# Retention and Fourier mixing on one core: the hand-ordered first batch reworked

## The chip, the cores and the metric

The kernel runs on one core of a Trainium2 chip. The metric is the device time of one execution in microseconds (us). The kernel before takes 272.87 us (median of three runs, 272.81 to 275.85).

## What is computed

Four batches, eight heads, 768 positions, head width 64. A retention layer is followed by a Fourier mixing layer and an MLP. The reference, cut:

```python
for t in range(S):                       # retention, per head, gamma = 1 - 2**(-5-h)
    state = gamma * state + outer(k[:, :, t], v[:, :, t])
    y[:, :, t] = scale * q[:, :, t] @ state
x = y as (batch, 768, 512)
u = x + real(fft(fft(x, axis=1), axis=2))
un = (u - mean(u)) / sqrt(var(u) + 1e-6)
out = u + relu(un @ w_ch1) @ w_ch2       # 512 -> 2048 -> 512
```

## The kernel before

**Retention.** The 768 positions are six chunks of 128 (`NCH`). Heads go in pairs, in the order of `PAIR_ORDER`. For each pair the kernel transposes q and k on TensorE, multiplies them chunk by chunk (`wkA`), applies the decay mask (`atm`), builds the states between chunks (`wkK`, `s16`), adds both parts in PSUM (`wkY`) and writes x as f16. Head columns 0 to 255 go to one side of `xts`, 256 to 511 mirrored to the other, with edge columns of zeros.

**Fourier mixing.** The two transforms are done as real products with cosine and sine tables. `fold_s` adds and subtracts the two halves of the positions (`xab`); `fold_d` adds and subtracts the two sides (`eo`, index e for sum and difference, cb for a half of the columns); `s1_unit` is the first DFT step (six matmuls for each e and cb, then one copy to `g`, on ACT or VectorE); `g0_unit` computes one extra column that is added as a scalar per row; `gr_unit` makes the mirrored copy `g16r`; `s2_unit` is the second DFT step for a block of 128 rows (kb 0 to 5). It leaves the cosine part (psP) and the sine part (psQ) in one PSUM bank, copies psQ to `qn` on ACT, combines them on VectorE into `u` (two instructions, L708 and L710), and adds x in two halves (L714, L717). Blocks 3 to 5 use the mirrored `g`. `norm_unit` subtracts the mean. For blocks 0 to 2 of batch 0 the mean comes from a sum of x (`xmean_unit`) and g0 (`mean_unit`), so that the statistics can wait.

**MLP.** `unT_unit` transposes the block (TensorE for batches 0 and 1, a DMA transpose for 2 and 3), `h_unit` (L778) or, for the first three blocks of batch 0, `h0_unit` (L795) is the first product with its ReLU, `ch_unit` (L815) the second. The MLP of one batch (the list `majors`) is interleaved with the retention and DFT of the next.

**What sets the order.** `first_units` is a list written by hand for batch 0's retention, DFT and first normalised blocks. After each of its units `pin()` ties every new instruction to the last one of its engine, so every engine runs the list in this order. After that `emit` merges streams of units, each with a start and an end on an axis on which the MLP of batch b covers b to b + 1. The units before 0.05 are pinned on all engines, the later ones on Pool alone; on the other engines the framework's scheduler orders them. `late_consts` (the masks `maskp`, eight ACT copies) is emitted between the two.

**Around the change.** On Pool the start sets decay constants (`gk5`, L185 and L287), edge columns (L277, L278) and casts q, k and v of each pair (L328, L337, L340, L353). `csn_unit` (L244) copies a cosine table for g0. `parity_consts` is six small VectorE instructions. `filler(n)` (L115) issues n matmuls on zeros to keep TensorE active. `sc_unit` is the scan over chunks (L425), `ae_unit` the masks (L401), `x0_unit` the write of x (L469). `load_unit(1, i, after)` lets batch 1's loads wait for a weight load. PSUM has five banks for most tiles (`ps_g`), two for the retention output (`ps_y`) and one for fillers (`ps_w`) in the first part; then three banks take the place of the last two for `psh` and `psc` (`ps_pm`).

## Time and profile before

| | us or share |
|---|---|
| time, median | 272.87 |
| profiled span | 270.6 |
| first MLP matmul (L795) starts | 41.2 |
| TensorE busy | 90% |
| VectorE busy | 70% |
| ScalarE (ACT) busy | 42% |
| GpSimd (POOL) busy | 29% |
| filler matmuls L115 | 41, 13.6 us |
| last load of batch 0 issued, landed | 14.9, 22.2 |

A row of the page's groups gives line, engine and operation, written and read tiles with shapes and count, then busy time and mean ns of one, then the idle time of the engine just before and what ended it. A line of the timeline starts with its start and its length; a group that was merged has a count (x4). A line of the waits gives who waited for whom, then total us, times and the longest. PEld is TensorE's weight load, SPq the queue from which loads and stores are issued.

### The profile page before, as it was taken

Reading aid. Unit: us, or ns where it says so; the run is one execution under the profiler, and the core shown is the slowest. Engines: PE = TensorE matmul, PEld = TensorE weight load, DVE = VectorE, ACT = ScalarE, POOL = GpSimd, SP = SyncE. Lnnn points to the kernel's source line nnn. Section 1 sums busy time; section 2 is a strip of 40 time slices with the busy share of each in tenths; the row PEclk is TensorE's granted clock in tenths of the full one; section 3 lists DMA queues with packets and bytes.
Section 4 is the critical chain, followed back from the end, with each engine's and each line's share of the span. In section 5 each row is a group of like instructions: output and inputs, shape, how many; then the busy total and the mean of one; then the engine's idle time right before and its main releaser. Section 6 shows DMA issues by size and latency. Waiting matters only on the chain.

```text
span 270.6 us, 5220 instructions
## 1 busy us (share of the span) xinstructions
PE 244.0 (90%) x2009; PEld 147.3 (54%) x2009; DVE 188.7 (70%) x447; ACT 114.0 (42%) x232; POOL 78.7 (29%) x138
## 2 busy tenths in 40 slices
PE   7785775989999989999997899999999999999994
PEld 2364554875666544666554544665566446545541
DVE  8996848599988874699776672798787725623421
ACT  4885456375464542356224540451144413502300
POOL 8987125556000053454000390170002401200000
PEclk9998589999999999999999999999999999999999
DMA  8999997999989985979983044159110231112012
GB/s 183 264 244 146 202 203 149 253 218 249 185 203 203 190 134 146 235 145 220 212 193 79 1 87 128 39 108 146 39 41 0 51 107 39 38 42 78 0 41 78
DMA packets 97432, 35.99 MB, mean 133 GB/s; under 512 B 88192, under 2 KB 94336, under 8 KB 97408
## 3 DMA queue, kind: packets, MB, share of 16 engines
q1 hardware_dynamic: 93184, 31.47, 55.9%
q0 software_dynamic: 4224, 4.19, 9.8%
q8 instruction: 16, 0.26, 0.4%
q14 instruction: 8, 0.07, 0.1%
HBM read 27.26 MB, written 6.29 MB: 124 GB/s over the span
## 4 chain that ended last, share of the span: by engine, by line
PE 48%; DVE 30%; ACT 6%; DMA 6%; POOL 5%; issue 3%; SPq 0%; POOLq 0%; ACTq 0%; DVEq 0%
PE psc L815 22%; PE psh L778 14%; DMA qTz<-q16z 4%; DVE bst L734 4%; POOL u L717 3%; PE ps L645 3%; DVE atm L401 3%; DVE u L708 2%; ACT x L591 2%; DVE ht L784 2%; DVE u L710 2%; DVE eo L618 1%; DVE tmp L233 1%; DMA v<-in_v_dram 1%; PE psh L795 1%
## 5 line engine op out<-in xcount | busy, mean ns | idle before, releaser
L815 PE MATMUL psc<-w,ht 128*128 128x512 f16 x384 | 90.1, 379 | 0.0
L778 PE MATMUL psh<-unT,w 128*128 128x384 f16 x448 | 83.3, 326 | 2.4 <-DVE ht L784 1.4
L778 PEld LDWEIGHTS <-w 128*128 128x128 f16 x448 | 42.7, 98 | 27.9 <-issue 4.9
L815 PEld LDWEIGHTS <-ht 128*128 128x128 f16 x384 | 36.6, 98 | 36.6
L782 ACT ACTIVATE ht<-psh 128x384 f16<-128x384 f32 x56 | 27.3, 488 | 56.6 <-PE psh L778 56.6
L714 POOL TENSOR_TENSOR u<-u,x 128x256 f32<-128x256 f32 x18 | 11.4, 634 | 125.6 <-DVE u L708 123.3
L819 DVE SCALAR_TENSOR_TENSOR ob<-psc,stats,u 128x512 f32<-128x512 f32 x24 | 17.9, 745 | 30.5 <-PE psc L815 30.5
L784 DVE TENSOR_SCALAR ht<-psh 128x384 f16<-128x384 f32 x56 | 30.7, 548 | 11.3 <-PE psh L778 11.2
L532 DVE TENSOR_TENSOR atm<-wkA,maskp 128x512 f16<-128x512 f32 x36 | 24.0, 681 | 1.0 <-PE wkA L530 1.0
L736 ACT ACTIVATE un<-u,stats 128x512 f16<-128x512 f32 x21 | 15.2, 722 | 18.4 <-DVE stats L735 13.9
L591 ACT ACTIVATE x<-wkY,gexp 128x384 f16<-128x384 f32 x24 | 12.7, 581 | 20.4 <-PE wkY L583 20.4
L734 DVE BATCH_NORM_STATS2 bst<-u 128x6 f32<-128x512 f32 x21 | 14.5, 691 | 7.6 <-POOL u L717 7.6
L717 POOL TENSOR_TENSOR u<-u,x 128x256 f32<-128x256 f32 x21 | 13.6, 646 | 15.4 <-DVE u L714 10.6
L558 DVE SCALAR_TENSOR_TENSOR s<-s,gk,wkK 128x128 f16<-128x128 f16 x48 | 16.3, 339 | 1.0
L708 DVE SCALAR_TENSOR_TENSOR u<-pq,g,qn 128x257 f32<-128x257 f32 x24 | 11.5, 477 | 5.9 <-ACT qn L705 5.9
L313 POOL TENSOR_SCALAR kd<-k,gexp 128x384 f16<-128x384 f32 x24 | 13.8, 585 | 4.8 <-DMA k<-in_k_dram 4.8
L795 PE MATMUL psh<-unT,w 128*128 128x128 f16 x192 | 11.9, 219 | 3.7 <-DVE ht L802 3.4
L115 PE MATMUL wps<-ht 128*128 128x512 f16 x41 | 13.6, 448 | 1.4 <-POOL ht L156 1.4
L795 PEld LDWEIGHTS <-w 128*128 128x128 f16 x192 | 11.2, 98 | 4.3 <-issue 4.2
L530 PE MATMUL wkA<-qTz,kT 128*128 128x256 f16 x72 | 13.3, 273 | 0.2
L311 ACT CAST q16z<-q 128x384 f16<-128x384 f32 x16 | 7.7, 513 | 10.9 <-DMA qTz<-q16z 10.9
L710 DVE SCALAR_TENSOR_TENSOR u<-pq,g,qn 128x255 f32<-128x255 f32 x24 | 11.2, 468 | 0.0
(138 smaller groups left out, 325.4 us busy)
## 6 DMA issues: line engine op xcount, KB each, us to landing
q<-in_q_dram SPq DMA_DIRECT2D x16, 384.0 KB, 6.1
k<-in_k_dram SPq DMA_DIRECT2D x16, 384.0 KB, 5.1
v<-in_v_dram SPq DMA_DIRECT2D x16, 384.0 KB, 6.0
out_dram<-ob SPq DMA_DIRECT2D x24, 256.0 KB, 2.3
w<-in_moe_w_ch_dram POOLq DMA_DIRECT2D x8, 512.0 KB, 10.9
unT<-un SPq DMA_TRANSPOSE x12, 2.4
qTz<-q16z SPq DMA_TRANSPOSE x8, 4.8
kT<-kd SPq DMA_TRANSPOSE x8, 2.8
```

Of the source, the lines that this page charges most:

```text
L532: nc.vector.tensor_tensor(out=st["atm"][:, 2 * part:2 * part + 2], in0=wk, in1=maskp[:, PAIR_ORDER[i]].unsqueeze(1).to_broadcast([P, 2, 2, ...
L591: nc.scalar.activation(dst, yk[h2], AF.Copy, bias=0.0, scale=gq8[:, h:h + 1])
L708: nc.vector.scalar_tensor_tensor(out=u[:, kb, 0:257], in0=psP, scalar=g0, in1=qn, op0=ALU.add, op1=op_lo)
L710: nc.vector.scalar_tensor_tensor(out=u[:, kb, 257:512], in0=psP[:, 255:0:-1], scalar=g0, in1=qn[:, 255:0:-1], op0=ALU.add, op1=op_up)
L717: eng.tensor_tensor(out=u[:, kb, 256:512], in0=u[:, kb, 256:512], in1=x[:, kb, 1, 257:1:-1], op=ALU.add)
L734: nc.vector.bn_stats(bst, u[:, kb, :])
L778: nc.tensor.matmul(psh, w116[:, cb, fb * P:(fb + 1) * P], unT[:, cb, rt * 384:(rt + 1) * 384], start=(cb == 0), stop=(cb == 3))
L782: nc.scalar.activation(ht16[:, fb, :], psh, AF.Relu, bias=0.0, scale=-1.0)
L784: nc.vector.tensor_scalar(out=ht16[:, fb, :], in0=psh, scalar1=-1.0, scalar2=0.0, op0=ALU.mult, op1=ALU.max)
L795: nc.tensor.matmul(psh[:, f], w116[:, cb, fb * P:(fb + 1) * P], unT[:, cb, kb * P:(kb + 1) * P], start=(cb == 0), stop=(cb == 3))
L815: nc.tensor.matmul(psc, ht16[:, fb, rb3 * P:(rb3 + 1) * P], w216[:, fb, :], start=(fb == 0), stop=(fb == NFB - 1))
L819: nc.vector.scalar_tensor_tensor(out=ob, in0=psc, scalar=lb[b]["st"][:, rb, 3:4], in1=lb[b]["u"][:, rb, :], op0=ALU.mult, op1=ALU.add)
```

## The change

It reworks the hand-written first batch and moves a few things in the streams:

- [...]The memsets of the decay constants `gk5` on Pool become ACT copies from a small VectorE table `gkrow` (which also takes the place of `gk128`). The zeros of `qTz` move from Pool to VectorE and later. `csn_unit` goes to a later place, the edge columns of the second x tile to the end of the list.
- **Residual of the first blocks on TensorE.** For blocks 0 to 2 of batch 0, `px_unit` adds x in the PSUM of the second DFT step: four matmuls with half an identity (`hid`, `nhid`), since psP + psQ and psP - psQ give both sides. The edge columns of `qn` get half of x by a small ACT copy. The adds L714 and L717 are gone for these blocks. For blocks 3 to 5 of batch 0 the adds move from VectorE to Pool.
- **g0 chain split.** `g0_unit` is in three parts: its input copies, its matmuls, its last two VectorE instructions, each in its own place.
- **Order.** `fold_d` is split by e, pair 3's masks for head 0 come ahead of the scan, more fillers stand there, means are taken per block, two mirror copies come earlier, the copy of g for e = 1 is always on VectorE.
- **Streams.** Batch 1's loads wait for the seventh weight load, not the eighth. Batch 1's retention starts at 0.27 of batch 0's MLP, not at 0.12. In all batches the first step's second columns and the second step are placed later. Pool is pinned only before 1.0.

The core of the diff:

```diff
     def gk_unit(hp):
         def run():
-            for h2 in range(2):
-                nc.gpsimd.memset(gk5[D * h2:D * h2 + D, hp, :, 1:NCH - 1],
-                                 float(gam[2 * hp + h2] ** P))
+            nc.scalar.copy(gk5[:, hp], gkrow[:, hp].unsqueeze(1).to_broadcast([P, D, NCH - 1]))
...
     def qt_zeros():
         for j in range(2):
-            nc.gpsimd.memset(qts[j][0:D, 1], 0.0)
-            nc.gpsimd.memset(qts[j][D:P, 0], 0.0)
+            nc.vector.memset(qts[j][0:D, 1], 0.0)
+            nc.vector.memset(qts[j][D:P, 0], 0.0)
...
+    def px_unit(kb):
+        def run():
...
+            pq = lb[0]["pq", kb] = (ps_y if kb < 2 else ps_g).tile(
+                [P, DM], f32, tag="y" if kb < 2 else "g", name="pq0")
+            x = xts[0][:, kb]
+            for n, (dst, half, side, lo, hi) in enumerate((
+                    (pq[:, 0:257], hid, 0, 1, 258), (pq[:, 0:257], hid, 1, 1, 258),
+                    (pq[:, 257:512], hid, 0, 2, 257), (pq[:, 257:512], nhid, 1, 2, 257))):
+                nc.tensor.matmul(dst, half, x[:, side, lo:hi], start=(n == 0), stop=False,
+                                 skip_group_check=True)
...
+            if early:
+                nc.scalar.activation(
+                    qn[:, 0:257:256],
+                    xts[0][:, kb].rearrange("p s d -> p (s d)")[:, 1:XW + 258:XW + 256],
+                    AF.Copy, bias=0.0, scale=0.5)
             nc.scalar.copy(qn[:, 1:256], psQ)
...
-            eng = nc.vector if b == 0 else nc.gpsimd
-            eng.tensor_tensor(out=u[:, kb, 0:256], ...)
-            eng = nc.vector if (b == 0 and kb >= 3) else nc.gpsimd
-            eng.tensor_tensor(out=u[:, kb, 256:512], ...)
+            if early:
+                return
+            nc.gpsimd.tensor_tensor(out=u[:, kb, 0:256], ...)
+            nc.gpsimd.tensor_tensor(out=u[:, kb, 256:512], ...)
...
-        un += a(3) + [kv0_unit(3), sc_unit(3)] + e(3, *heads)
-        un += [yx_unit(3), filler(1), yi_unit(3, 0), x0_unit(3, 0), yi_unit(3, 1), x0_unit(3, 1),
-               t_act(4, 1), t_act(4, 2)]
-        un += [fold_s(0, 0, 130, 1, 2), fold_d(0, 0), g0_unit(0), s1_unit(0, 0, 0),
-               s1_unit(0, 1, 0), filler(2), xmean_unit(0)]
-        un += [fold_s(0, 130, 258, 1, 2), fold_d(0, 1), s1_unit(0, 0, 1), s1_unit(0, 1, 1),
-               filler(2), xmean_unit(1), xmean_unit(2), mean_unit]
-        un += [s2_unit(0, 0), s2_unit(0, 1), norm_unit(0, 0), filler(6), unT_unit(0, 0),
-               s2_unit(0, 2), norm_unit(0, 1), norm_unit(0, 2)]
-        un += [gr_unit(gi) for gi in range(4)] + [gk_late]
+        un += a(3) + e(3, (0, 0), (1, 0)) + [kv0_unit(3), filler(3), sc_unit(3),
+               t_act(4, 0), t_act(4, 1)]
+        un += e(3, (0, 1), (1, 1))
+        un += [yx_unit(3), yi_unit(3, 0), x0_unit(3, 0), filler(2), yi_unit(3, 1), x0_unit(3, 1),
+               g0_unit(0, (1,))]
+        un += [fold_s(0, 0, 130, 1, 2), fold_d(0, 0, (0,)), s1_unit(0, 0, 0), t_act(4, 2),
+               fold_s(0, 130, 258, 1, 2), fold_d(0, 0, (1,)), fold_d(0, 1, (0,)), px_unit(0),
+               xmean_unit(0), fold_d(0, 1, (1,)), s1_unit(0, 1, 0), s1_unit(0, 0, 1),
+               s1_unit(0, 1, 1), px_unit(1), filler(1), g0_unit(0, (2,)), mean_unit(0)]
+        un += [s2_unit(0, 0), s2_unit(0, 1), norm_unit(0, 0), gr_unit(0), gr_unit(1),
+               px_unit(2), filler(4), unT_unit(0, 0), xmean_unit(1), mean_unit(1),
+               norm_unit(0, 1), s2_unit(0, 2), xmean_unit(2), mean_unit(2), norm_unit(0, 2),
+               gr_unit(2), gr_unit(3), edge_zeros, x_edges(1)]
...
-            pin(None if e[0] < 0.05 else ["Pool", "GpSimd"])
+            if e[0] < 1.0:
+                pin(None if e[0] < 0.05 else ["Pool", "GpSimd"])
...
-                streams.append(([load_unit(1, i, 7) for i in range(4)], -0.1, 0.0))
-                streams.append(([qt_zeros], 0.02, 0.05))
+                streams.append(([load_unit(1, i, 6) for i in range(4)], -0.1, 0.0))
+                streams.append(([qt_zeros], 0.1, 0.15))
                 streams.append(([pad_unit], 0.9, 0.95))
-                ts = (0.12, 0.22, 0.24, 0.33, 0.42, 0.52, 0.59, 0.67)
+                ts = (0.27, 0.31, 0.34, 0.42, 0.51, 0.60, 0.67, 0.74)
...
-                ts = [0.04 + 0.58 * sum(n[:j]) / sum(n) for j in range(7)]
+                ts = [0.04 + 0.57 * sum(n[:j]) / sum(n) for j in range(7)]
...
-            streams.append((mix_units(b + 1, [0, 1, 2]), b + ts[-1], b + ts[-1] + 0.15))
+            streams.append(([s1_unit(b + 1, 0, 1), s1_unit(b + 1, 1, 1)], b + ts[-1] + 0.04,
+                            b + ts[-1] + 0.06))
+            streams.append((mix_units(b + 1, [0, 1, 2]), b + ts[-1] + 0.09, b + ts[-1] + 0.24))
```

## The prediction

> **What bounds the kernel now.** I read the page's busy shares and slices first, then TensorE's waits on both sides of 47 us, then the timeline of the stretches with the long waits. The page:
>
> ```profile
> PE 244.0 (90%) x2009; PEld 147.3 (54%) x2009; DVE 188.7 (70%) x447; ACT 114.0 (42%) x232; POOL 78.7 (29%) x138
> PE   7785775989999989999997899999999999999994
> PEclk9998589999999999999999999999999999999999
> ```
>
> A slice is 6.8 us. From the eighth on PE is at nine tenths or more nearly throughout; the first seven are looser, and only there does the granted clock fall. PE's waits before 47 us, then after 47 us:
>
> ```profile
> PE wkY L456 <- DVE s L425: 1.8, 2, 1.4
> PE pst L765 <- ACT un L730: 1.5, 1, 1.5
> PE ps L671 <- DVE xg L666: 1.5, 1, 1.5
> ```
>
> ```profile
> PE psh L795 <- DVE ht L802: 3.4, 1, 3.4
> PE pq L699 <- ACT g L650: 1.6, 1, 1.6
> PE pst L765 <- ACT un L736: 1.6, 3, 0.7
> ```
>
> So two regimes. Up to 47.8 us a dependency chain sets the time: loads, four head pairs, folds, DFT steps, first MLP matmul at 41.2. After it PE has work ahead; adding the idle of 5 us windows from 50 us on gives 8.0 us, of which only the waits above can be touched. The longest is in the timeline of 42 to 48 us:
>
> ```profile
> 42.56 3.73 DVE L658 COPY g16r<-g 128x384 f16<-128x384 f16 x4
> 43.08 0.73 POOL L207 MEMSET qTz<- 64x768 f16 x1
> ...
> 43.80 1.69 ACT L197 ACTIVATE maskp<-maskf 128x128 f32<-128x128 f32 x8
> ...
> 45.39 1.05 ACT L800 ACTIVATE ht<-psh 128x512 f16<-128x512 f32 x2
> ...
> 47.01 0.69 DVE L802 TENSOR_SCALAR ht<-psh 128x512 f16<-128x512 f32 x1
> 47.76 2.45 PE L795 MATMUL psh<-unT,w 128*128 128x128 f16 x41 [3.41 <-DVE ht L802]
> ```
>
> PE has filled three psh buffers and stands until VectorE, in its fixed order, is through four mirror copies and eight small memsets. The copies are slow:
>
> ```profile
> L654 DVE COPY g16r<-g x12: 247/261/264, 87.3 to 205.9; 128x384 f16<-128x384 f16 x12
> L658 DVE COPY g16r<-g x4: 867/869/1364, 42.6 to 45.4; 128x384 f16<-128x384 f16 x4
> ```
>
> The same copy takes 261 ns later, and 869 ns here, while Pool sets qTz.
>
> **What the Trainium skill says.** "SBUF — State Buffer", section "SBUF: two separate sides": VectorE in a two-port mode (or reading two SBUF tensors, against a Pool operation that reads) and Pool take one port pair as a lock for a whole instruction, the other blocks. The two rows agree: 261 against 869 ns. "TensorE: Matmul & The Clock Gate", Part 1: PE's clock halves after a window of about 3.4 us with too little activity, and comes back after a busy one. The trace agrees: the clock is 0.50 from 26 to 35 us after a thin stretch (PE busy 0.42, 0.30 and 0.76 in the windows at 22, 24 and 25 us), and six DFT matmuls take 1.07 to 1.18 us there against 0.67 at 138 us. How many fillers hold it, neither says.
>
> **The change part by part.**
>
> Start, 0 to 21 us. Off Pool go the gk memsets (0.76 + 1.53 + 1.48 us) and the csn copies; two ACT copies of 320 elements (about 0.45 us each, from 0.52 for 386) run before ACT's first trig input is there (5.14 now). The casts can then follow the loads (now kd of pair 0 waits for the gk memsets till 7.8, though k0 landed at 5.8), but loads set the last pair: k3 was issued at 14.35 and landed 6.8 us later, at 21.2; v3 at 22.2. DMA is busy at 1.0 or more throughout. Casting earlier brings pair 0 about 1.2 us and pair 1 about 1 us forward, and nothing of it survives at pair 3. The parity constants (2.2 us at 9.45) move ahead of pair 2's masks; VectorE has 2.1 us of idle before pair 3, which hides them. I cost this part at 0.
>
> Pair 3, 21 to 30 us. More fillers (ten for two between 22 and 29 us, 0.21 us each, in PE's idle time) push its kT by up to 0.4 us; head 0's two masks ahead of the scan let yi of head 0 go earlier. I put pair 3's last x at 29.9, as before (29.95). Gain 0.
>
> Folds and first DFT step, 30 to 36 us. Before, VectorE did fold 0.62, both differences 1.03, the g0 chain to 31.6, then fold 0.62 and 1.03, ending 33.2. Now one difference (0.52) comes ahead of the second fold, and the g0 copies are done long before: 29.95 + 0.62 + 3 x 0.52 = 32.1. So the last difference is 1.1 us earlier. PE's four groups of six cost 0.55 us each at full clock instead of 1.1. Four residual matmuls of 257 or 255 columns are added per block; PE streams 512 columns in 216 ns (48 in 10.36 us), so about 0.11 each, 0.45 a block, 1.3 in all, on a PE which waits for VectorE here. Last group 32.15 to 32.75, px(1) and a filler to 33.45 beside the copy of g (0.59), second step's matmuls done 34.0, against 36.8. **Gain 2.85 us if the clock holds; about 0 if it doesn't** (four groups at 1.1 and px at 0.9 a block end where they did). The nearest bounds on an unseen thing are these two. I take the first: the fillers between 22 and 29 us go from 0.4 to 2.1 us of PE work.
>
> Second step to first MLP matmul. Before: second-step matmuls end 36.8, first transpose 40.1, so 3.3 us. Gone are the VectorE add (0.41) and Pool's add with its handover (0.85); new is a two-element ACT copy per block (nearest rows 0.19 to 0.29; I take 0.2, behind PE's work). That leaves 2.4, and four fillers of 0.86 end ahead of it. Transposes at 36.4, first MLP matmul 37.5, against 41.2: 3.7 us by here.
>
> The stall at 44 us. Mirror copies 0 and 1 go earlier, 2 and 3 cost 0.26 each, the gk128 memsets (0.77) are gone, qTz memsets leave Pool for VectorE later (four of 0.22 to 0.43; the 192-word memset took 0.22). PE fills three buffers by 40.3. VectorE frees its one at about 42.0. The other two wait for ACT, which has un of block 1 (to 39.1), block 2's copies (39.7), the mean of block 2 (0.81), un (to 41.5), eight maskp copies (1.69, to 43.2) and then ht, to 43.8. So PE gets one group at 42.0 and stays busy from 43.9; before, the same group started at 47.76 and the one after it at 48.7. **Gain 4.8 us in all**: the stall does not go, ACT inherits 3.6 us of the gap; the gain is nearly all the 3.7 from above plus 1.1 here.
>
> Batch 0's later blocks: six adds of 0.41 to 0.66 leave VectorE for Pool at 0.64 each. Pool's order puts them ahead of batch 1's casts, whose loads now start when the seventh weight load has landed, about 42 instead of 44.8. Hidden while PE has MLP work. Batch 1's attention starts at 0.27 of the batch instead of 0.12 and ends at 0.74; VectorE, 89% busy from 50 to 95 us, takes its 26 us (per pair three mask products of 0.68, four state steps of 0.34, 0.28 and 0.96 of copies, 18.6 for four; some 7.5 of folds and g copies) in a narrower space. Slack: batch 1's last un was ready at 104, its first MLP matmul ran at 108.6. I cost it at 0, with 3 us as upper bound.
>
> Room between steps. Second columns' first step and the second step come 0.04 and 0.08 of a batch later. What it can recover is PE idle near these steps: 1.0 us at 95 to 105, 3.1 at 135 to 160, 0.9 at 200 to 215. The middle one:
>
> ```profile
> 147.75 0.51 ACT L311 CAST q16z<-q 128x384 f16<-128x384 f32 x1 [2.68 <-DMA qTz<-q16z]
> ...
> 148.95 0.59 ACT L650 CAST g<-ps 128x386 f16<-128x386 f32 x1
> ...
> 149.60 0.28 PE L699 MATMUL pq<-cd,g 128*128 128x257 f16 x1 [1.64 <-ACT g L650]
> ```
>
> The copy of g stands on ACT behind a cast that waits for a DMA transpose; spacing doesn't remove the cast. Of 5.0 us I take a quarter, 1.2; bounds 0 and 3.
>
> Sum: 4.8 + 1.2 = 6.0, so 272.9 - 6.0 = **266.9 us**.
>
> **Rivals.**
> Clock still drops: 2.85 us of the first part go, and half the room is gained: 272.9 - 2.0 - 0.6 = 270.3. For it: how much activity holds the clock is not shown. Against it: eight more fillers.
> VectorE or loads take it back in batch 1: loads start only 2.8 us earlier, so 4.8 falls to 2.8, and the compressed attention gives no room: 270.1. For it: VectorE's 89%. Against it: 4.6 us of slack at 104.
> Larger: all three DFT stalls go (3 of 5) and ACT's 3.6 us gap half closes because the order of maskp and ht differs: 272.9 - 4.8 - 3.0 - 1.6 = 263.5.
> Slower: Pool's order is no longer pinned from batch 1 on, so casts for the next batch may stand ahead of residual adds and wait for loads. One such wait is in the chain already (DMA of v, 3.79 us at 116.3, ahead of an add at 120.1). If it hit the two adds of three blocks, at two places in three batches, 6 x 3.8 = 23 less half hidden behind MLP work, less 4.8: 272.9 + 6.6 = 279.5. For it: ACT, not pinned, shows it at 147.75. Against it: the pinned order has the wait too, and PE lost only 0.2 us at 120.
>
> **How the numbers follow.** Forecast 0.50, clock 0.14, given back 0.12, larger 0.15, slower 0.09. Faster by over 2% means below 267.4: most of the forecast (0.42) and the larger case, 0.57. Slower by over 2% is 0.08. The rest 0.35. Range: from the larger case, 263.0, to above both cases of 270, 270.8; outside are the slower case and some of each end.
>
> **What would show it.** Right: clock 1.00 through 26 to 36 us; first MLP matmul at 37 to 38 us; mirror copies near 260 ns; PE's next long wait on ACT's ht behind maskp; idle after 50 us some 7 us. Wrong: clock 0.50 at 30 us; first MLP matmul after 40; a PE wait on Pool or un at a batch's start above 3 us; casts ahead of adds on Pool in batches 1 to 3.

## The result and the profile after

| | before | after | difference |
|---|---|---|---|
| time, median (range) | 272.86 (272.81 to 275.85) | 265.06 (264.46 to 265.88) | ratio 0.969, 95% interval 0.963 to 0.975 |
| profiled span | 270.6 | 263.0 | -7.6 |
| first MLP matmul starts | 41.17 | 39.48 | -1.7 |
| batch 0's last output written by VectorE, start | 108.64 | 103.52 | -5.1 |
| the same of batch 3 | 266.62 | 259.03 | -7.6 |

Two runs of the comparisons below, one of the kernel before (360.27 us) and one of the first batch alone (356.32 us), ran at a granted clock of about 0.65 and are left out of the ranges and ratios.

The change makes the kernel 3.1% faster. Of the 7.6 us of span, 1.7 are gained before the first MLP matmul, 3.4 between it and the end of batch 0, and 2.5 in the three batches after. The page after, its busy shares and slices:

```profile
PE 242.4 (92%) x2020; PEld 148.1 (56%) x2020; DVE 184.2 (70%) x446; ACT 115.9 (44%) x238; POOL 75.1 (29%) x132
PE   7497799979999998999999999999999999999993
PEclk9898899999999999999999999999999999999999
```

The PE row reads nine tenths from the sixth slice on, with gaps in the ninth and the sixteenth; before, it had gaps up to the 23rd. But the clock row has an 8 in the second, fourth and fifth slices: the clock was not held throughout, and the loss in the second slice is new. TensorE's waits of the kernel after, before 42 us and then after 42 us (columns: who waits for whom, us in total, times, longest):

```profile
PE wkA L404 <- ACT kT L390: 2.8, 1, 2.8
...
PE ps L659 <- DVE eo L628: 0.9, 1, 0.9
...
PE wkY L466 <- DVE s L435: 0.9, 2, 0.5
```

```profile
PE pst L816 <- ACT un L787: 2.3, 2, 1.4
PE psh L829 <- DVE ht L835: 1.6, 4, 0.7
PE psh L829 <- ACT ht L833: 1.0, 2, 0.6
```

Both long waits of before, the 3.4 us for VectorE's `ht` and the 1.6 us for ACT's `g`, are missing from the second list. The longest wait of the first list, 2.8 us for the `kT` of pair 0, is new; it comes back below under the start. The place where TensorE stood from 44.3 to 47.8 us looks like this after (timeline: start, length, engine, line, operation):

```profile
42.16 0.39 PE L816 MATMUL pst<-ident,un 128*128 128x128 f16 x4
42.24 0.42 DVE L672 COPY g16r<-g 128x384 f16<-128x384 f16 x2
42.38 0.39 PE L744 MATMUL pq<-cd,g16r 128*128 128x257 f16 x2
42.59 0.68 DVE L853 TENSOR_SCALAR ht<-psh 128x512 f16<-128x512 f32 x1
42.99 1.69 ACT L194 ACTIVATE maskp<-maskf 128x128 f32<-128x128 f32 x8
43.32 1.05 PE L846 MATMUL psh<-unT,w 128*128 128x128 f16 x16
...
44.38 0.39 PE L744 MATMUL pq<-cd,g16r 128*128 128x257 f16 x2
44.58 1.06 ACT L851 ACTIVATE ht<-psh 128x512 f16<-128x512 f32 x2
45.20 3.01 PE L846 MATMUL psh<-unT,w 128*128 128x128 f16 x51
```

Two mirror copies take 0.42 us together, where before four took 3.73. ACT's `ht` still stands behind the eight `maskp` copies, at 44.58, but TensorE has other work until then: one MLP group, transposes and second-step matmuls (L816, L744). In the 6.59 us after the first MLP matmul TensorE is busy 6.34 us; before it was 3.18.

### The profile page after: what moved, and what is told of

It is laid out like the page before. It is cut to its first block, busy times and chain, and to the rows that moved or that the text cites. A ratio compares the mean times of both kernels' runs of the same rounds, so it can differ in the third digit from the quotient of the medians.

```text
span 263.0 us, 5235 instructions
## 1 busy us (share of the span) xinstructions
PE 242.4 (92%) x2020; PEld 148.1 (56%) x2020; DVE 184.2 (70%) x446; ACT 115.9 (44%) x238; POOL 75.1 (29%) x132
## 4 chain that ended last, share of the span: by engine, by line
PE 56%; DVE 24%; ACT 8%; POOL 6%; issue 3%; DMA 1%; POOLq 0%; ACTq 0%; DVEq 0%
PE psc L866 23%; PE psh L829 19%; DVE bst L785 4%; POOL u L769 3%; PE ps L659 3%; DVE u L760 3%; POOL u L767 2%; PE wkA L540 2%; DVE ht L835 2%; PE wps L115 2%; DVE atm L411 2%; DMA qTz<-q16z 1%; DVE s L568 1%; DVE eo L628 1%; DVE atm L542 1%
## 5 line engine op out<-in xcount | busy, mean ns | idle before, releaser
L829 PEld LDWEIGHTS <-w 128*128 128x128 f16 x448 | 42.8, 98 | 26.8 <-issue 3.4
L767 POOL TENSOR_TENSOR u<-u,x 128x256 f32<-128x256 f32 x21 | 13.4, 637 | 93.3 <-DVE u L760 90.9
L870 DVE SCALAR_TENSOR_TENSOR ob<-psc,stats,u 128x512 f32<-128x512 f32 x24 | 17.9, 746 | 28.1 <-PE psc L866 28.0
L785 DVE BATCH_NORM_STATS2 bst<-u 128x6 f32<-128x512 f32 x21 | 14.5, 693 | 7.7 <-POOL u L769 7.7
L568 DVE SCALAR_TENSOR_TENSOR s<-s,gkrow,wkK 128x128 f16<-128x128 f16 x48 | 16.4, 341 | 1.3
L115 PE MATMUL wps<-ht 128*128 128x512 f16 x40 | 14.2, 467 | 1.4 <-POOL ht L156 1.4
L769 POOL TENSOR_TENSOR u<-u,x 128x256 f32<-128x256 f32 x21 | 13.4, 636 | 2.5 <-DVE u L762 1.9
L328 POOL TENSOR_SCALAR v<-v 128x768 f16<-128x768 f32 x12 | 10.0, 832 | 10.7 <-PE wkY L593 8.8
L757 ACT COPY qn<-pq 128x255 f32<-128x255 f32 x24 | 8.9, 371 | 6.9 <-PE pq L748 6.9
```

What stands on the lines that cost most here:

```text
L115: nc.tensor.matmul(wps, wz[:, 0:P], wz, start=True, stop=True)
L568: nc.vector.scalar_tensor_tensor(out=s16[:, c], in0=s16[:, c - 1], scalar=gkrow[:, hp, 1:2], in1=wk[:, c - c0], op0=ALU.mult, op1=ALU.add)
L767: nc.gpsimd.tensor_tensor(out=u[:, kb, 0:256], in0=u[:, kb, 0:256], in1=x[:, kb, 0, 1:257], op=ALU.add)
L769: nc.gpsimd.tensor_tensor(out=u[:, kb, 256:512], in0=u[:, kb, 256:512], in1=x[:, kb, 1, 257:1:-1], op=ALU.add)
L785: nc.vector.bn_stats(bst, u[:, kb, :])
L829: nc.tensor.matmul(psh, w116[:, cb, fb * P:(fb + 1) * P], unT[:, cb, rt * 384:(rt + 1) * 384], start=(cb == 0), stop=(cb == 3))
```

## The experiments

The experiments ran in three groups, each on one chip: the four that came first (first batch, streams, adds back, cosine copies), the three with the cast behind together with the repeat of the first batch, and the last four. The kernel after was timed before them, on a chip that isn't known. So a comparison with its 265.06 us, or between groups, is one across chips, and the text says so where it matters. The kernel before scatters by some us from run to run (269.6 to 277.2 on the first group's chip), so kernels are compared by medians with their ranges, and by the ratio to before, measured on the same chip, where it says more. "First batch" means the rework of the hand-written list, "streams" the later starts, the room between steps and the pin.

### The first batch alone

```diff
-                streams.append(([load_unit(1, i, 6) for i in range(4)], -0.1, 0.0))
-                ts = (0.27, 0.31, 0.34, 0.42, 0.51, 0.60, 0.67, 0.74)
+                streams.append(([load_unit(1, i, 7) for i in range(4)], -0.1, 0.0))
+                ts = (0.12, 0.22, 0.24, 0.33, 0.42, 0.52, 0.59, 0.67)
...
-            if e[0] < 1.0:
-                pin(None if e[0] < 0.05 else ["Pool", "GpSimd"])
+            pin(None if e[0] < 0.05 else ["Pool", "GpSimd"])
```

(and the DFT steps where they were before). The second of these is the same kernel again, for its trace.

> The changed kernel with the streams of before (places of the second batch's retention, of the second columns and the second DFT step, pins of Pool, start of batch 1's loads); only the first batch's list is new. Theory A (the prediction: most of the gain is the first batch, and what is won there is kept): 4.8 us under the kernel before, 268.1 us. Rival B (the first batch gains little, since batch 1's loads and VectorE take it back, and the gain is in the streams): 271 us or more. By the two traces, the end of batch 0 came 5.1 us earlier; if that needs the later start of batch 1's retention, this run stands between the two.

> A second look at the changed first batch with the streams of before, for its trace. Theory A: MLP of batch 0 starts as in the changed kernel, at 39.5 us, and no wait of 3.4 us follows; the 4 to 5 us won are then lost at the turn from batch 0 to batch 1, where ACT's cast of batch 2's q stands ahead of the sine copies or VectorE is late. Rival B: they are lost at once, since batch 1's retention starts before its loads are there, so PE stands between 50 and 65 us for casts.

Measured: 271.01 us (269.25 to 271.84), ratio 0.995, interval 0.993 to 0.998; the second time 270.81. The first MLP matmul is at 38.09, 3.1 us earlier than before and even earlier than in the kernel after; yet batch 0 ends at 108.85, as before (108.64). So a gain of 3.1 us and the stall's 3.4 us are lost again inside batch 0. The timeline of this kernel, 49 to 59 us (in brackets the idle time of the engine just before and what ended it):

```profile
49.16 0.83 POOL L314 TENSOR_SCALAR q16z<-q 128x768 f16<-128x768 f32 x1 [2.76 <-DMA q<-in_q_dram]
...
54.03 0.83 POOL L328 TENSOR_SCALAR v<-v 128x768 f16<-128x768 f32 x1 [2.02 <-DMA v<-in_v_dram]
54.83 0.64 POOL L767 TENSOR_TENSOR u<-u,x 128x256 f32<-128x256 f32 x1
...
56.09 0.69 DVE L785 BATCH_NORM_STATS2 bst<-u 128x6 f32<-128x512 f32 x1 [6.72 <-POOL u L769]
...
58.40 0.61 PE L816 MATMUL pst<-ident,un 128*128 128x128 f16 x4 [3.81 <-ACT un L787]
```

Pool waits for a load of batch 1 to cast q, then k, then v, and only then comes the residual add of block 4 of batch 0. VectorE's statistics wait 6.72 us for that add, TensorE 3.81 us for the block; and then the clock falls. The windows of the same kernel (columns: window, length, busy us of PE, PEld, DVE, ACT, POOL with counts, granted clock, DMA share, GB/s):

```profile
48.00:52.00 4.00, 2.55 (x40) 2.18 (x37) 1.37 (x3) 1.49 (x3) 1.96 (x3) 1.00 1.29 254
52.00:56.00 4.00, 2.52 (x42) 2.35 (x42) 0.00 (x0) 0.00 (x0) 1.98 (x4) 1.00 1.17 251
56.00:60.00 4.00, 1.16 (x9) 0.88 (x9) 3.52 (x9) 2.38 (x4) 2.08 (x5) 0.64 1.02 231
60.00:64.00 4.00, 3.41 (x20) 2.19 (x19) 3.76 (x12) 3.39 (x7) 4.00 (x8) 0.51 1.19 256
```

From the first MLP matmul to the end of batch 0 this kernel takes 6.7 us longer than the kernel after. Of these, 4.5 are idle time of TensorE (8.0 against 3.55 us after the first 6.59), and 2.2 are the same matmuls at the lower clock. What the trace suggests: the adds of blocks 3 to 5, which the change moved to Pool, are only free because batch 1's retention starts later. In the kernel after the same adds stand ahead of the first cast (46.6 to 53.8 us), and the cast comes right behind them. The run puts loads, starts, room and pin back together; the start alone was not tried.

### The streams alone

The kernel before, with the new starts, room, load and pin (the reverse of the diff above) and the later place of the zeros of `qTz`.

> The kernel before with the new streams and the old first batch. Theory A: the room between the steps is worth 1.2 us (prediction) to 2.9 us (what the traces show between the ends of batch 0 and batch 1), so 270 to 271.7 us. Rival B: 268 us or less, the streams being the larger half. Sum check: if the two halves do not influence each other, the gains of this run and of the run with only the first batch add up to 7.8 us.

Measured: 271.98 us (269.97 to 274.79), ratio 0.999, interval 0.996 to 1.002: nothing. The stall at 44 us is there as before, `PE psh L795 <- DVE ht L802: 3.4`, and at the start of batch 1 there is a new loss. The timeline of this kernel:

```profile
99.27 0.92 ACT L311 CAST q16z<-q 128x384 f16<-128x384 f32 x2 [2.44 <-DMA q<-in_q_dram]
...
100.10 0.64 ACT L705 COPY qn<-pq 128x255 f32<-128x255 f32 x2
...
104.36 0.40 PE L765 MATMUL pst<-ident,un 128*128 128x128 f16 x4 [1.79 <-ACT un L736]
```

ACT stands 2.44 us for a load of batch 2's q, with the sine copies of batch 1's second step, ready since 98, behind it. "PSUM — Partial Sum Buffer", section "Engine vs sequencer instructions", of the Trainium skill calls the queues of ACT, VectorE and Pool strict FIFO; this trace agrees, to the cost of 2.44 us. From the last copy of g to the first `un` of batch 1 it takes 6.6 us here (97.03 to 103.59), and 4.5 us both before (94.94 to 99.40) and after (92.53 to 97.00).

So the two halves bring 1.4 and 0.4 us apart (against 272.38, the median of before on their chip), and 7.8 together. By these numbers each takes away what stops the other; how much of that is only the order on ACT, the experiments with the cast behind tell.

### The residual back on VectorE and Pool

The kernel after without `px_unit`, `half_ids` and the edge copies: blocks 0 to 2 of batch 0 are added as before the change.

```diff
-            early = b == 0 and kb < 3
+            early = False
...
-            nc.gpsimd.tensor_tensor(out=u[:, kb, 0:256], ...)
+            eng = nc.vector if (b == 0 and kb < 3) else nc.gpsimd
+            eng.tensor_tensor(out=u[:, kb, 0:256], ...)
```

> The changed kernel with the residual of the first three blocks added as before: one add on VectorE and one on Pool for each block, no residual matmuls and no half identities, edge columns of zeros. Theory A (the adds lay on the chain to the first MLP matmul, 0.41 plus 0.85 us less 0.2 for the edge copy, and the residual matmuls ran in PE's idle time): 1.0 us slower, 266.1 us, first MLP matmul at 40.5. Rival B (the residual matmuls, 0.45 us a block, delay the first DFT step as much as the adds cost): no change, 265.1 us.

Measured: 271.26 us (268.45 to 273.66), ratio 0.996, interval 0.993 to 0.999; the profiled run took 268.58. The runs fall into two groups, near 269 and near 272, and the cause of that spread stays open. The number by itself would say that the residual on TensorE brings 4 to 6 us. The trace says something else: the first MLP matmul is at 39.66, only 0.2 later than after. From there 1.6 us are lost to the clock, which falls to 0.50 from 39.6 to 43.0 us (the first 48 MLP matmuls take 4.43 us, after 2.84), and the larger loss is at 95 us, far from any edit. This kernel first, then the kernel after, both at the start of batch 1's second step:

```profile
95.41 0.93 ACT L321 CAST q16z<-q 128x384 f16<-128x384 f32 x2 [2.61 <-DMA q<-in_q_dram]
96.24 0.63 ACT L757 COPY qn<-pq 128x255 f32<-128x255 f32 x2
96.64 0.49 DVE L760 SCALAR_TENSOR_TENSOR u<-pq,g,qn 128x257 f32<-128x257 f32 x1 [2.75 <-ACT qn L757]
```

```profile
93.49 0.37 ACT L757 COPY qn<-pq 128x255 f32<-128x255 f32 x1 [1.17 <-PE pq L748]
93.90 0.49 DVE L760 SCALAR_TENSOR_TENSOR u<-pq,g,qn 128x257 f32<-128x257 f32 x1 [0.49 <-ACT qn L757]
...
94.40 0.93 ACT L321 CAST q16z<-q 128x384 f16<-128x384 f32 x2 [0.53 <-DMA q<-in_q_dram]
```

On ACT, which is not pinned here, the scheduler put the cast ahead of the copies in one kernel and behind the first of them in the other. The source at this place is the same. The comparison is spoiled by an order that nobody wrote; so the next three kernels fix it.

### The cast put behind the copies, in three kernels

The first line stands ahead of ACT's cast of q for the next batch.

```diff
+                    es.enter_context(tc.issue_after(lb[b - 1]["qn"].ins))
...
-            nc.scalar.copy(qn[:, 1:256], psQ)
+            qc = nc.scalar.copy(qn[:, 1:256], psQ)
+            if kb == 2:
+                lb[b]["qn"] = qc
```

One on the kernel with the adds back, one on the kernel after, one on the streams alone.

> The kernel with the adds back, with one more order on ACT: a batch's q casts (batches 2 and 3) are issued behind the last sine copy of the second DFT step of the batch before. In the trace of the adds-back kernel the cast of batch 2's first q stood ahead of batch 1's sine copies and waited 2.6 us for its load, to 95.4 us; the first un of batch 1 came 6.7 us after the last copy of g, 4.5 in the changed kernel, where the cast stands behind the first of them. Theory A (this order on ACT, which the scheduler happened to choose, is what the adds-back kernel lost beyond the adds): first un 4.5 us after g again, batch 0 ends about 2 us earlier, 266.5 to 269 us against 268.5 to 271.7. Rival B (the adds themselves, through the late and slow start of the MLP, cost it): time as with the adds back.

> The changed kernel with the same order on ACT: q casts of batches 2 and 3 behind the last sine copy of the batch before. Theory A (the cast is the lottery ticket of all versions): here the first cast already stands behind the first sine copy, so batch 0 to 1 gains at most 0.5 us; at 142.0 us a cast of batch 3 waits 1.4 us ahead of the copy of g, and PE then stands 0.7 us, so 0.5 to 1.2 us faster in all, 264.2 us. Rival B (casts that come later make the DMA transposes of the next batch late): 1 us or more slower, with PE waits on kT or qT at the starts of batches 2 and 3.

> The kernel before with the new streams and this order on ACT. In the run with the streams alone, the cast of batch 2's q stood ahead of batch 1's sine copies and waited 2.4 us for its load, and PE then waited 1.8 us for un. Theory A: the streams' gain was there and was given back by this order; with the cast behind, 2 us faster than the streams alone, 269.5 us. Rival B (the streams are worth nothing without the new first batch, for another reason): 271.5 us.

Measured:

| kernel | cast as scheduled | cast behind |
|---|---|---|
| adds back | 271.26, ratio 0.993 to 0.999 | 266.26 (265.74 to 268.03), 0.967 to 0.982 |
| streams alone | 271.98, ratio 0.996 to 1.002 | 269.08 (268.56 to 269.85), 0.977 to 0.991 |
| after | 265.06, ratio 0.963 to 0.975 | 264.97 (264.41 to 266.94), 0.962 to 0.980 |

In the first two rows the intervals of the ratio don't overlap: the cast's place is worth 2 to 5 us there (the two profiled spans of the first row differ by 2.2; the two columns ran on different chips). In the kernel after it is worth nothing, since the scheduler had left it in a harmless place: from the last copy of g to the first `un` it takes 4.5 us there, against 6.7 with the adds back, 5.3 after the edit to that, and 4.5 after the edit to the streams. With the order fixed, on one chip, the streams without the new first batch are at 269.08 us, where the kernel before has 273.94 (271.47 to 275.43), and on top of them the new first batch takes off another 4.1 us (264.97; the ranges don't overlap). So the streams alone do bring something (ratio 0.977 to 0.991) once the cast is out of the way; the new first batch brings more on top of them than alone (1.4 us), for which the first experiment's trace gives the reason. The residual on TensorE comes to 266.26 - 264.97 = 1.3 us, where the prediction had 0.41 + 0.85 - 0.2 = 1.06. But the ranges overlap, and the clock differs between the two profiled runs (lost at 23.3 to 26.7 us with the adds back, at 11.6 to 15.0 after), so this gain isn't shown.

### The cosine copies earlier

After the change `csn_unit` runs on Pool beside VectorE's first fold. The timeline of the kernel after:

```profile
24.08 2.46 DVE L618 TENSOR_TENSOR xab<-x 128x774 f16<-128x774 f16 x2
24.16 2.02 POOL L241 TENSOR_SCALAR csn<-csp 128x384 f16<-128x384 f16 x3
```

The fold took 1.01 us before. This experiment moves the copies ahead:

```diff
-               filler(1)] + x(0) + [v0_unit(1), half_ids]
+               filler(1)] + x(0) + [v0_unit(1), csn_unit(0), csn_unit(1), half_ids]
```

(the third one behind `v0_unit(2)`).

> The changed kernel with the three copies of the cosine table for g0 back at their places of before. In the changed kernel's trace they run on Pool from 24.2 to 26.2 us, beside the first fold on VectorE, which takes 2.46 us for two there against 1.01 before. Theory A (the copies and the fold block each other, and pair 3 is late by this): the fold back at 1.0 us, the last x of pair 3 at about 30.5 instead of 31.9 us, first MLP matmul at about 38, time 263.7 us. Rival B (the fold has slack, ACT or the slow clock hold pair 3): fold faster, but first MLP matmul within 0.4 us of 39.5 and time unchanged at 265.1.

The fold in this kernel:

```profile
24.35 1.01 DVE L618 TENSOR_TENSOR xab<-x 128x774 f16<-128x774 f16 x2
```

Measured: 265.16 us (265.04 to 265.40), first MLP matmul 39.75. The fold is back to 1.01 us, and the time doesn't move. The change had put a new collision on the port pair, of a VectorE operation with two SBUF inputs and a Pool operation that reads SBUF, just what "SBUF — State Buffer", section "SBUF: two separate sides", describes; it costs 1.45 us of VectorE and nothing that these times show. In both profiled runs the clock fell at 24.7 to 24.8 us, and pair 3's masks wait for TensorE. Where the clock holds there, in the trace with blocks 3 to 5 later (further down), the fold takes 2.82 us, and TensorE waits 0.93 us for the cast of v that VectorE has behind it; what the collision costs then was not tried.

### The pin, the room, the fillers, the place of the blocks

The four kernels of this part share a chip, but not with the kernels that they are compared to. Pool pinned everywhere, as before, in the kernel after (`pin(...)` without `if e[0] < 1.0`):

> The changed kernel with Pool's order pinned in all batches, as before. Theory A (the free order on Pool helps: with the pin, adds of batch 1 stand behind casts that wait for loads, as at 112 to 120 us in the kernel before): 1 to 2 us slower, 266 to 267 us, with batch 1's end late by that. Rival B (the free order is what the slower rival of the prediction feared, or it is worth nothing): 265.1 us or less.

Measured: 265.69 us (265.11 to 266.01). The kernel after has 265.06 (264.46 to 265.88), and the ratios to before are 0.974 to 0.979 here and 0.963 to 0.975 there: the ranges overlap, so a cost of the pin isn't shown. The inside differs more: first MLP matmul at 37.85, end of batch 0 at 105.31, so 1.6 earlier and then 1.8 later than after. Why batch 0 took longer was not followed up.

The room between steps taken out, cast behind as above (the first step's second columns with the fold again, the second step at the end of step 5, without + 0.09):

> The changed kernel with q casts behind (the earlier run at 265.0 us, so that ACT's order is not left to chance), and the places of the second columns and of the second DFT step of before (no room). Theory A (the room keeps PE from waiting on the copies of g and on un): 1.2 to 2.9 us slower, 266.2 to 267.9 us, with PE waits on g at the second steps. Rival B (what looked like the worth of the room was the order of ACT's casts): 265.0 us, within 0.5.

Measured: 265.31 us (264.76 to 266.36), against 264.97 (264.41 to 266.94) with the room. Nothing that these runs can tell.

Eight fillers fewer around pair 3:

```diff
-        un += [yx_unit(2), fold_s(0, 0, 258, 0, 1), g0_unit(0, (0,)), k0_unit(3), filler(2),
-               x0_unit(2, 0), t0_unit(3, 1), te_unit(3, 1), x0_unit(2, 1), filler(3),
+        un += [yx_unit(2), fold_s(0, 0, 258, 0, 1), g0_unit(0, (0,)), k0_unit(3),
+               x0_unit(2, 0), t0_unit(3, 1), te_unit(3, 1), x0_unit(2, 1), filler(1),
...
-        un += a(3) + e(3, (0, 0), (1, 0)) + [kv0_unit(3), filler(3), sc_unit(3),
+        un += a(3) + e(3, (0, 0), (1, 0)) + [kv0_unit(3), filler(1), sc_unit(3),
...
-        un += [yx_unit(3), yi_unit(3, 0), x0_unit(3, 0), filler(2), yi_unit(3, 1), x0_unit(3, 1),
+        un += [yx_unit(3), yi_unit(3, 0), x0_unit(3, 0), yi_unit(3, 1), x0_unit(3, 1),
```

> The changed kernel with the fillers around pair 3 as few as before: 2, 1, 1 and none in place of 2, 2, 3, 3 and 2 there. Theory A (the fillers hold the clock): clock at 0.50 for 6 us or more between 25 and 36 us, DFT groups of six at 1.1 us, first MLP matmul at 40 to 41 us, 1.5 to 2.5 us slower, 267 us. Rival B (the phase of the clock's window decides, or the residual matmuls and the denser order hold it alone): cold stretch of 3 us or none, time within 0.6 of 265.1.

Measured: 265.92 us (264.97 to 267.19). In the profiled run, the slowest of the four, the clock was 0.50 from 27.4 to 37.7 us, as long as in the kernel before (25.4 to 35.6), and the first MLP matmul came at 41.46. The fastest run has 264.97, as good as after. The times alone don't decide between theory A and rival B. One more trace helps: that of the next experiment has all the fillers in the same hand-written list, and runs within 0.1 us of this one up to the masks of pair 2 (20.62 against 20.66 us). From 24.0 to 27.4 us TensorE is busy 2.24 us there and the clock stays; with few fillers it is busy 1.35 us and the clock falls. So in this pair the fillers hold the clock. The kernel after lost it with all of them, so they don't always.

Blocks 3 to 5 of batch 0 spread over more of the MLP, cast behind:

```diff
-                    (mix_units(b, [3, 4, 5]), b + (0.12 if b == 0 else 0.02), b + 0.3)]
+                    (mix_units(b, [3, 4, 5]), b + (0.12 if b == 0 else 0.02),
+                     b + (0.42 if b == 0 else 0.3))]
```

> The changed kernel with q casts behind, and batch 0's blocks 3 to 5 spread to 0.42 of the batch in place of 0.30. In the changed kernel PE stands 1.4 us at 56 us for the un of block 5, which isn't needed before the second half of the MLP; PE idle from 52 to 60 us is 1.4 us. Theory A (only the place is wrong): 1.0 us faster than 265.0, 264.0 us. Rival B (VectorE and Pool are full there, and the work that comes later meets batch 1's casts and masks): no change or slower, with PE waits on masks or casts between 60 and 90 us.

Measured: 267.28 us (266.09 to 267.45), 1.4 to 2.0 us over the three others of its chip, and 2.3 over its base, the kernel after with the cast behind (264.97, on another chip). TensorE's waits of this kernel after 42 us begin with

```profile
PE tq L497 <- POOL q16z L314: 1.9, 1, 1.9
PE pst L819 <- ACT un L790: 1.4, 1, 1.4
```

Batch 1's casts stand behind the adds of block 5, as in the kernel after, but the adds come later: the first cast starts at 56.2 us, not at 53.8, and TensorE has to wait for it (until 57.1 us). At 58.1 us the clock falls for 3.4 us. The order of Pool has two sides: adds that wait behind casts in the first experiment, casts that wait behind late adds here. The kernel after lies between them. None of these kernels beats it.

## Why the prediction was right

The forecast of 266.9 us (263.0 to 270.8) met 265.06: faster, and by 7.8 us where 6.0 were forecast. Its sum was 4.8 by the end of the stall and 1.2 after. Measured are 5.1 by the end of batch 0 and 2.5 after. The first number is nearly right by luck, through two errors of opposite sign. Of the signs that the prediction named for "right", the mirror copies came (0.21 us each). The clock was at 0.50 until 28.1 us, the first MLP matmul came at 39.48, the wait for ACT's `ht` behind `maskp` did not come, and TensorE's idle time from 50 to 260 us is 8.0 us, as before.

**Start and pair 3, cost 0: wrong by 0.8 to 2.0 us.** The last x of pair 3 is written at 31.94, not at 29.9. One failing step is that of the parity constants: "VectorE has 2.1 us of idle before pair 3, which hides them". That idle lies at 24 to 26 us, behind the point through which the path runs. The kernel before at this point, and then the kernel after with the cast behind, whose clock is full here:

```profile
20.12 1.95 DVE L401 SCALAR_TENSOR_TENSOR atm<-wkA,maskf 128x384 f16<-128x384 f32 x4
20.72 0.49 PE L369 MATMUL tq<-ident,q16z 128*128 128x128 f16 x6 [0.22 <-DVE atm L401]
21.25 0.80 ACT L377 COPY qTz<-tq 128x768 f16<-128x768 f16 x1 [0.46 <-PE tq L369]
```

```profile
21.21 0.15 DVE L220 TENSOR_SCALAR sgn<-odd 128x1 f32<-128x1 f32 x1
21.27 1.94 DVE L412 SCALAR_TENSOR_TENSOR atm<-wkA,maskf 128x384 f16<-128x384 f32 x4
21.87 0.49 PE L380 MATMUL tq<-ident,q16z 128*128 128x128 f16 x6 [0.67 <-DVE atm L412]
22.40 0.80 ACT L388 COPY qTz<-tq 128x768 f16<-128x768 f16 x1 [0.56 <-PE tq L380]
```

The last parity constant ends just as the masks of pair 2 begin, 1.15 us later than before; pair 3's transposes wait for these masks and are 1.15 us later, and so is the copy of `qTz`. Some of it is won back (head 0's masks now come ahead of the scan), and the last x is written at 30.7 in that kernel, 0.8 over the forecast. That is read from the traces and was not tried alone. (The loads, which the forecast had busy "at 1.0 or more throughout", are at 0.90 and 0.80 of the DMA from 20 to 22 us; nothing hangs on it.)

Not all of the 1.15 us is the constants. The other failing step is that of the start: pair 0 was to come 1.2 us earlier, with nothing lost on the way. In the kernel after:

```profile
11.20 0.82 PE L404 MATMUL wkA<-qTz,kT 64*128 64x128 f16 x12 [2.77 <-ACT kT L390]
```

TensorE waits 2.77 us for the `kT` of pair 0, which stands on ACT behind the table functions, and these start 1.2 us later than before (6.36 against 5.18 us). Their input comes from VectorE, which first has the new table of decay constants (0.77 us) and two of the `qTz` zeros (0.38 us each, at 1.35 and 2.57 us): VectorE isn't pinned for these zeros, and the scheduler put them there. So pair 0's first masks come at 11.82 us, before at 11.58. Then the clock falls: it is 0.50 from 11.0 to 14.5 us here and from 11.6 to 15.0 with the cast behind, and the kernel before has no such loss. Pair 1's masks are 0.6 us late in both (16.66 and 16.67, before 16.06). In the trace with blocks 3 to 5 later the clock holds: there pair 1's masks are 0.5 us early (15.52) and pair 2's 0.5 us late (20.62, before 20.12), with the six constants, 1.0 us in all, between them. So the constants cost about 0.9 us at this point, and in the kernel with the cast behind the early loss of the clock goes with some 0.6 us more. The other two `qTz` zeros didn't come later either: they run on VectorE at 26.68 and at 31.43 us, the last one just ahead of the first difference; what they cost was not tried.

The 1.2 us between the kernel after (31.94) and the same kernel with the cast behind (30.7) go mainly with the second loss of the clock.

**The clock, "gain 2.85 us if it holds": it held where it was priced, and fell just before.** One-microsecond windows of the kernel after, then of the same kernel with the cast behind, whose hand-written first batch is the same list:

```profile
23.00:24.00 1.00, 0.64 (x13) 0.47 (x10) 1.00 (x2) 0.94 (x2) 1.00 (x2) 1.00 1.22 203
24.00:25.00 1.00, 0.78 (x11) 0.45 (x11) 1.00 (x2) 0.22 (x1) 0.97 (x3) 0.85 0.62 40
25.00:26.00 1.00, 1.00 (x7) 0.65 (x6) 1.00 (x2) 0.36 (x1) 1.00 (x2) 0.50 0.51 66
...
30.00:31.00 1.00, 1.00 (x19) 0.63 (x17) 1.00 (x4) 0.25 (x1) 0.61 (x1) 1.00 1.29 218
```

```profile
23.00:24.00 1.00, 0.42 (x11) 0.27 (x8) 1.00 (x3) 0.72 (x2) 1.00 (x2) 1.00 1.23 205
24.00:25.00 1.00, 1.00 (x14) 0.63 (x14) 1.00 (x2) 0.45 (x1) 0.97 (x3) 1.00 0.52 75
25.00:26.00 1.00, 1.00 (x10) 0.43 (x7) 0.85 (x3) 0.70 (x2) 1.00 (x3) 1.00 0.63 58
```

Counts in brackets left out, the clock is the sixth number after the length. It drops to 0.50 for 3.4 us in the first, from 24.7 us, and stays full in the second. The first DFT step ran at full clock in both: six matmuls in 0.67 to 0.69 us, against 1.07 to 1.18 before. From pair 3's last x to the first MLP matmul it took 7.54 us (31.94 to 39.48), and 7.5 with the cast behind (30.7 to 38.23); forecast 37.5 - 29.9 = 7.6; before 11.2. The term has two parts: to the end of block 0's second step and from there to the first transposes; they gained 2.5 and 1.1 us, forecast 2.85 and 0.9. So this term of the sum, 3.7 us, was right, and the 1.7 us that the first MLP matmul is earlier are these 3.7 less the 2.0 us that pair 3 came late.

**The stall, "ACT inherits 3.6 us of the gap": wrong, in the good direction.** ACT is late, as forecast: `ht` at 44.58, 5.1 us after the first MLP matmul; forecast 43.2 - 37.5 = 5.7. But apart from one group the gap was counted as empty. It holds that MLP group in VectorE's freed buffer, the transposes of blocks 1 and 2, and second-step matmuls of blocks 3 and 4, which need mirror copies: these are done at 42.7 now, at 46.3 before, where TensorE's next instruction after 44.07 was an MLP group that had to wait for `ht`. TensorE's idle time in the 6.59 us from the first MLP matmul falls from 3.41 to 0.25: 3.2 us instead of the 1.1 forecast. The same 0.25 is found with the cast behind, where the MLP begins 1.25 us sooner, so it isn't owed to the late start. No run moves the mirror copies, or the memsets on Pool beside them, alone; that they closed the stall is read from the two traces.

**Pool's adds and the later start, cost 0: right as a sum, wrong as a reason.** From there to the end of batch 0 TensorE idles 3.55 us, 2.97 before: 0.6 us lost, within the bound of 3. But the later start was treated as a cost that is hidden. By the first experiment's trace it is what makes the adds on Pool possible: without the new streams 6.7 us are lost between the first MLP matmul and the end of batch 0 (38.09 to 108.85 is 70.8 us, 64.0 in the kernel after). That is the mechanism of the rival "slower", casts that wait for loads ahead of adds, in the batch where nobody looked for it, and in the pinned order, not for want of a pin.

**Room between steps, 1.2 us: right in size, not shown as the cause.** After batch 0 the idle time of TensorE falls from 5.1 to 3.7 us, by 1.4; in a further 1.1 us of the 2.5 TensorE is busy less, with the same 1074 matmuls of the same kinds, and why stays open. The wait for g at 149 us is gone. But without the room the time is the same within the ranges, and with only the first batch changed the part after batch 0 is short too (156.3 us; before 158.0, after 155.5). The forecast said "spacing doesn't remove the cast", and the cast is still there:

```profile
142.00 0.93 ACT L321 CAST q16z<-q 128x384 f16<-128x384 f32 x2 [1.43 <-DMA qTz<-q16z]
143.21 0.59 ACT L664 CAST g<-ps 128x386 f16<-128x386 f32 x1
```

TensorE no longer waits for g, since MLP groups lie between; but g's copy still starts 0.8 us after its matmuls end (at 142.43), and TensorE then waits 0.71 us, at 145.1, for an `ht` that VectorE does after its copies of g. Which of the moves in the order helped stays open.

**The rivals.** "Clock still drops" happened twice for 3.4 us, at 11.0 and 24.7 us; other runs of the same list have one loss up to the first MLP matmul, or none. Between the kernel after and the one with the cast behind the second loss goes with 1.2 us up to the MLP. In the time of the whole kernel it doesn't show: with the cast behind batch 0 ends 0.9 us earlier than after (102.61), and the last output is only 0.2 us earlier. "VectorE or loads take it back" didn't happen, though blocks 3 to 5 placed a little later bring it up. "Larger" at 263.5 was right in closing the stall further and was not reached, since pair 3 came late.

## What to carry to other kernels

Idle time hides added work only if it lies between the added work and the next step of the path, so follow the buffer or the order through which the path runs before an edit is costed at nothing. Before work is moved to another engine's queue, read what stands ahead of it there and whether that waits for a load: the same adds cost nothing in one order, and in another TensorE stood 3.8 us for them and lost its clock. And where a scheduler chooses the order, an experiment may differ from its base at a place that the edit never touched; look for it in the trace, fix that order, and only then believe the difference.

## What the runs showed of the hardware

- The clock of TensorE is not a function of the instruction list. With the same hand-written list it fell to 0.50 at 24.7 to 28.1 us in the profiled run of the kernel after, and stayed at 1.00 there in those of the kernel after with the cast behind, with Pool pinned, without the room, with blocks 3 to 5 later, and of the first batch alone; the first MLP matmul then came at 39.5 or at 37.9 to 39.0. The early loss, between 11 and 16 us, is in all of these but the one with blocks 3 to 5 later.
- In the 13 traces other than that of the 356 us run every loss ahead of the last output lasted 3.4, 6.8 or 10.2 us: one, two or three times 3.41. Where one trace has two losses, their starts lie a multiple of 3.41 us apart (11.04 and 24.70 in the kernel after, 4 times; 12.32 and 39.62 with the adds back, 8 times), and from run to run they lie elsewhere (11.04, 11.62, 12.37). So the clock looks as if it were set anew every 3.41 us, at moments that differ from run to run. "TensorE: Matmul & The Clock Gate", Part 1, says that the window is free-running and that the number of cold matmuls is run-variable; the runs agree, and between the kernel after and the one with the cast behind about 1.2 us go with it. TensorE's busy time in the 3.41 us ahead doesn't decide it alone: the clock fell after 0.80 and after 2.13 us (kernel after, at 11.04; before, at 25.38), and stayed after 1.60 (blocks 3 to 5 later, at 10.34).
- A VectorE fold with two f16 inputs in SBUF took 1.01 us alone (two instructions) and 2.46 us beside Pool copies that read SBUF, 1.37 to 2.83 in the nine traces that have them side by side; a single-input f16 copy took 0.26 us alone and 0.87 us beside a Pool memset. In the kernel after and the kernel before these are 2.4 and 3.3 times as long without any wait being listed for them.
